# Fewer and longer tiled w4 excursions, padded kv and M products, earlier pq transposes and a longer filler in a matmul-bound mixer kernel

## Chip, cores and metric

One core of one Trainium2 chip. The metric is the device time of one execution in microseconds (us), and the median over the runs is quoted. Engines: PE is TensorE (PEld its weight loads), DVE is VectorE, ACT is ScalarE, POOL is GpSimd, SP issues most DMAs. The profile traces one execution; its span (263.0 us before) is about 2 us shorter than the device time.

## The reference, cut

```python
x = A_x                                            # (1, 2048, 640) bf16
g = sigmoid((x * gate_w).sum(-1, keepdims=True))
# A: linear attention, 32 heads of 20
q, k, v = split(x @ wqkv); pq, pk = phi(q), phi(k)
kv = einsum("bhsd,bhse->bhde", pk, v); z = pk.sum(s)
a = (pq @ kv / (pq . z)) @ wo
# B: token-shift mixer and an MLP of width 1728
h  = gelu(layernorm(x) @ w1); x1 = x + shift(h) @ w2
b  = x1 + gelu(layernorm(x1) @ w3) @ w4
return g * a + (1 - g) * b
```

The sequence is 16 tiles of 128 tokens. The MLP width 1728 is 13 x 128 + 64. Those last 64 rows are the "w4 half": a product that contracts over 64 rows only.

## The kernel before, the parts that matter

The program is recorded by items (`("w3", c, j)` and so on). A small scheduler in Python puts the items in order by a model of time and by stated dependencies; each engine then executes its own list in that order. The 64-row products for two token tiles run at once, one on each half of the array's rows:

```python
    def w4_half(t):                        # called for even t: tiles t and t+1
        ...
        for i in range(2):
            b = pair()                     # two of the eight PSUM banks per tile
            bs += [b, b + 1]
            w4_banks[t + i] = (b, b + 1)
        bank_hold.update(bs)
        for i, (n0, n1) in enumerate(((0, 512), (512, D))):
            for par in range(2):
                rows = slice(64 * par, 64 * par + 64)
                jobs.append((ps[:, bs[2 * par + i], 0:n1 - n0],
                             h2h[rows, t // 4, 128 * pr:128 * (pr + 1)], w4[rows, KFF, n0:n1]))
        ...
    # kvt_group: for the last of six blocks both the stationary and the moving side have 40 columns
    m = min(128, D - R6 * r)               # 128, ..., 40
    mms.append((ps[0:m, b, ...], wv[:, k, R6 * r:R6 * r + m], GT[:, k, R6 * r:R6 * r + n], ...))
    # m_group: the last of six blocks contracts 40 rows, the others 120
    mm_group(ps[:, b, 0:512], [(Lt[0:n, r, :], wo_aug[0:n, r, 0:512])])
    # transposes of the normalized pq tiles: only after the last transpose of xn
    IT.add("QT", ("qt", t), 0.0, ..., deps=[(("qn", t), 3.2), (("w2", NT - 1), 0.5), (("t2", NT - 1), 0.0)])
    # filler products before x arrives, so that the PE clock is released
    NWARM = 5; NWARM2 = 2                  # 512 columns each
```

`w3_half` is the matching 64-column product of w3 (two for the whole sequence). Each w4 tile is followed by an eviction on DVE that adds it to `abx`, which an A tile (`a_tile`, product of pq and M) wrote before.

## Time and profile before

| | before |
|---|---|
| device time, median (range, 6 runs) | 264.98 us (264.82 to 265.63) |
| span of the profiled run | 263.0 us |
| PE busy | 258.2 us, 98% |
| DVE, ACT, POOL busy | 56%, 41%, 35% |

The page of the kernel before: the span, the busy time of each engine, and the chain of work that ended last.

```profile
span 263.0 us, 4293 instructions
PE 258.2 (98%) x1699; PEld 134.9 (51%) x1699; DVE 146.8 (56%) x249; ACT 108.7 (41%) x217; POOL 93.1 (35%) x148
...
PE 88%; DMA 3%; POOL 3%; DVE 3%; ACT 1%; issue 1%; SPq 0%; DVEq 0%; POOLq 0%
```

PE has almost no slack, and nothing else is near it. The list of PE's waits confirms that (who waited for whom: total us, times, longest).

```profile
PE ps L835 <- POOL ones_c L666: 1.6, 1, 1.6
PE ps L607 <- DMA pqnT<-pq_tok: 0.3, 1, 0.3
PE ps L618 <- DMA x_tok<-in_A_x_dram: 0.2, 1, 0.2
```

But the busy time hides small holes, because the traced end of a product reaches into the next one. **Read start to start instead.** In a steady stream a 128x512 product starts 0.216 us before its follower and a 128x128 product 0.056 us before. The PE timeline of the kernel before (start us, duration us, engine, line, operation, names, tile, shape, count; a row merges neighbours of one line and shows the shape of the first), at the kv block, at the 40-row M product, and at the first A tiles with the first w4-half:

```profile
79.33 0.65 PE L937 MATMUL ps<-GT,wv 128*128 128x120 bf16 x10
79.92 2.33 PE L607 MATMUL ps<-xnT,w 128*128 128x512 bf16 x10
...
113.86 0.44 PE L607 MATMUL ps<-wo_aug,Lt 40*128 40x512 bf16 x2
114.23 1.96 PE L607 MATMUL ps<-w,hsT 128*128 128x512 bf16 x12
...
140.09 4.25 PE L607 MATMUL ps<-M_sb,pqnT 128*128 128x512 bf16 x30 [0.31 <-DMA pqnT<-pq_tok]
144.28 0.45 PE L1089 MATMUL ps<-w,h2h 64*128 64x512 bf16 x4
144.65 7.24 PE L1107 MATMUL ps<-w,h2T 128*128 128x512 bf16 x52
```

Fifteen A pairs take 15 x (0.216 + 0.056) = 4.08 us, so the w4-half should start at 144.17; it starts at 144.28. Its four products run as two concurrent pairs, 0.27 us of work; the next group should start at 144.55 and starts at 144.65. So there is a hole of about 0.1 us on the way into the 64-row tiles and another on the way out. The waits list shows neither. The PEld timeline of the kernel before shows the weight load of the new tile at the same place:

```profile
144.27 0.11 PEld L1089 LDWEIGHTS ps<-w,h2h 64*128 64x128 bf16 x4
```

In the steady stream a weight load starts 214 ns (median) before its product, beside the product ahead. Here it starts only 4 ns before its product, 94 ns after the columns of the product ahead have gone through. At all 24 changes of shape in this trace the load is held back like this (by 90 to 95 ns), and the product follows within 5 ns. So the hole is a pause ahead of both, not the time of an uncovered weight load; what goes on in the pause the trace does not show. The 40-row M product takes 0.37 us for 0.27 us of work, with one more hole ahead of it, and the kv block 0.59 us.

### The profile page before, as it was taken

To read this page: it belongs to the slowest core of one execution; us is meant where nothing else is said; L and a number is where in the kernel's file an instruction comes from. 1 tells how busy PE (TensorE), PEld (TensorE's weight loads), DVE (VectorE), ACT (ScalarE), POOL (GpSimd) and SP (SyncE) were. 2 spreads that over 40 slices of the span, in tenths; PEclk is the share of its full clock that TensorE was granted. 3 is DMA by queue.
4 is the path that set the end of the run, shared out by engine and by line. 5 is a ranking of instruction groups with operands and counts; after the bars stand their busy time and mean duration, and the time that the engine had idled before them with its cause. 6 is when DMAs were issued, how large, how long until landed. Compare 5 with 4: busy or idle time off the path is not lost.

```text
span 263.0 us, 4293 instructions
## 1 busy us (share of the span) xinstructions
PE 258.2 (98%) x1699; PEld 134.9 (51%) x1699; DVE 146.8 (56%) x249; ACT 108.7 (41%) x217; POOL 93.1 (35%) x148
## 2 busy tenths in 40 slices
PE   7999999999999999999999999999999999999996
PEld 3555555555555555554444554544555455545553
DVE  0497877899703797989995659611212121212242
ACT  3596677741365757775862013112221222121000
POOL 4013995859764027587861103001120011021020
PEclk9999999999999999999999999999999999999999
DMA  6775989641668896245256651410000200002011
GB/s 212 238 102 140 189 165 159 189 89 27 96 120 110 276 376 106 54 78 78 56 99 124 98 107 25 122 30 0 2 0 0 102 0 0 2 0 100 2 50 50
DMA packets 50675, 24.82 MB, mean 94 GB/s; under 512 B 42036, under 2 KB 49245, under 8 KB 50656
## 3 DMA queue, kind: packets, MB, share of 16 engines
q1 hardware_dynamic: 49408, 21.28, 36.5%
q0 software_dynamic: 1152, 3.28, 5.5%
q8 instruction: 13, 0.21, 0.3%
q14 instruction: 6, 0.05, 0.1%
q10 hardware_dynamic: 96, 0.00, 0.0%
HBM read 12.05 MB, written 2.62 MB: 56 GB/s over the span
## 4 chain that ended last, share of the span: by engine, by line
PE 88%; DMA 3%; POOL 3%; DVE 3%; ACT 1%; issue 1%; SPq 0%; DVEq 0%; POOLq 0%
PE ps L607 53%; PE ps L1107 22%; PE ps L787 8%; PE ps L859 2%; POOL xn L629 1%; DMA x_tok<-in_A_x_dram 1%; PE ps L1089 1%; POOL st L637 1%; DMA pqnT<-pq_tok 1%; DMA xnT<-xn 1%; DVE x_tok L644 1%; PE ps L618 1%; ACT junk L662 1%; PE ps L937 1%; PE ps L860 1%
## 5 line engine op out<-in xcount | busy, mean ns | idle before, releaser
L607 PE MATMUL ps<-xnT,w 128*128 128x512 bf16 x360 | 84.4, 379 | 0.0
L663 ACT ACTIVATE h2T<-ps 128x512 bf16<-128x512 f32 x52 | 31.0, 597 | 85.6 <-PE ps L607 85.6
L1107 PE MATMUL ps<-w,h2T 128*128 128x512 bf16 (+1 forms) x416 | 58.7, 299 | 0.0
L607 PEld LDWEIGHTS ps<-xnT,w 128*128 128x128 bf16 x360 | 33.4, 98 | 33.8 <-ACT M_sb L663 0.4
L629 POOL TENSOR_SCALAR abx<-x_tok,stg 128x640 f32<-128x640 bf16 x16 | 13.3, 834 | 104.5 <-DVE x_tok L646 72.7
L1107 PEld LDWEIGHTS ps<-w,h2T 128*128 128x128 bf16 x416 | 32.4, 98 | 27.8 <-issue 2.1
L646 DVE SCALAR_TENSOR_TENSOR x_tok<-ps,stg,abx 128x640 bf16<-128x640 f32 (+2 forms) x17 | 14.3, 844 | 49.2 <-PE ps L1107 49.2
L629 POOL TENSOR_SCALAR xn<-x_tok,st 128x640 bf16<-128x640 bf16 x32 | 35.5, 1115 | 8.8 <-DMA xnT<-xn 8.3
L646 DVE SCALAR_TENSOR_TENSOR abx<-ps,stg,abx 128x640 f32<-128x640 f32 x16 | 14.1, 883 | 29.4 <-PE ps L607 24.4
L663 ACT ACTIVATE Er<-ps 128x640 bf16<-128x640 f32 x32 | 22.5, 705 | 12.7 <-PE ps L607 8.5
L663 ACT ACTIVATE hsT<-ps 128x512 bf16<-128x512 f32 (+1 forms) x32 | 18.9, 594 | 14.6 <-PE ps L607 14.2
L662 ACT ACTIVATE junk<-x_tok 128x640 bf16<-128x640 bf16 x32 | 23.6, 737 | 1.5 <-DVE x_tok L644 1.2
L607 PE MATMUL ps<-M_sb,pqnT 128*128 128x512 bf16 (+1 forms) x160 | 23.7, 299 | 0.3 <-DMA pqnT<-pq_tok 0.3
L607 PE MATMUL ps<-w,hsT 128*128 128x512 bf16 (+1 forms) x160 | 23.9, 299 | 0.0
L787 PE MATMUL ps<-pk_tok,x_tok 128*128 128x512 bf16 (+1 forms) x160 | 23.9, 299 | 0.0
L607 PE MATMUL ps<-wkg,xT 128*128 128x512 bf16 (+1 forms) x150 | 22.6, 299 | 0.0
L607 PEld LDWEIGHTS ps<-M_sb,pqnT 128*128 128x128 bf16 x160 | 13.1, 98 | 12.8 <-DMA pqnT<-pq_tok 0.8
L607 PEld LDWEIGHTS ps<-w,hsT 128*128 128x128 bf16 x160 | 13.3, 98 | 12.4 <-DVE qprod L637 0.3
L607 PE MATMUL ps<-wq,xT 128*128 128x512 bf16 (+1 forms) x120 | 18.3, 299 | 0.0
L629 DVE TENSOR_SCALAR Er<-Er 128x640 bf16<-128x640 bf16 x32 | 12.0, 376 | 9.4 <-ACT Er L663 8.9
L644 DVE SCALAR_TENSOR_TENSOR x_tok<-ps,x_tok 128x640 bf16<-128x640 f32 x16 | 13.0, 821 | 7.4 <-PE ps L607 5.9
L607 PEld LDWEIGHTS ps<-wkg,xT 128*128 128x128 bf16 x150 | 12.1, 97 | 9.0
(67 smaller groups left out, 229.2 us busy)
## 6 DMA issues: line engine op xcount, KB each, us to landing
w<-in_B_w_dram SPq DMA_DIRECT2D x1, 2160.0 KB, 8.2
w<-in_B_w_dram SPq DMA_DIRECT2D x1, 2080.0 KB, 13.8
x_tok<-in_A_x_dram SPq DMA_DIRECT2D x3, 640.0 KB, 5.8
out_dram<-x_tok SPq DMA_DIRECT2D x3, 640.0 KB, 3.2
w<-in_B_w_dram POOLq DMA_DIRECT2D x8, 160.0 KB, 4.9
wq<-in_A_wqkv_dram SPq DMA_DIRECT2D x5, 160.0 KB, 4.3
wkg<-in_A_wqkv_dram SPq DMA_DIRECT2D x5, 160.0 KB, 4.2
wv<-in_A_wqkv_dram POOLq DMA_DIRECT2D x1, 800.0 KB, 6.5
```

What stands on the lines that cost most here:

```text
L607: ins = e.matmul(out_ap, l, r, start=(i == 0), stop=(i == n - 1))
L618: ins = e.transpose(o, s_, ident[:])
L629: return engf(lambda e: e.tensor_scalar(out_ap, in_ap, s1, s2, op0, op1), rd, [out_ap], cost=cost)
L637: return engf(lambda e: e.tensor_tensor(out_ap, a, b_, op), [a, b_], [out_ap], cost=cost)
L644: return dve(lambda e: e.scalar_tensor_tensor(out_ap, in0, scalar, in1, op0, op1, accum_out=accum), rd, [out_ap, accum], cost=cost + 70.0)
L646: return dve(lambda e: e.scalar_tensor_tensor(out_ap, in0, scalar, in1, op0, op1), rd, [out_ap], cost=cost)
L662: return act(lambda e: e.activation(out_ap, in_ap, func, bias=bias, scale=scale, accum_out=accum), rd, wr, cost=cost)
L663: return act(lambda e: e.activation(out_ap, in_ap, func, bias=bias, scale=scale), rd, wr, cost=cost)
L787: ins = e.matmul(o, l, r, start=(t0 + q_ == 0), stop=(t0 + q_ == NT - 1))
L859: e.matmul(ps[:, b, 0:512], l, w[:, k, 0:512], start=(k == 0), stop=(k == KD - 1))
L860: return e.matmul(ps[:, b + 1, 0:n2], l, w[:, k, 512:512 + n2], start=(k == 0), stop=(k == KD - 1))
L1107: ins = e.matmul(o, l, r, start=False, stop=(i == KFF - 1))
```

## The change

The intent is to take holes out of the PE stream: half as many changes between full and tiled products, no wait before the first A tile, and a filler that runs until x arrives. The diff, cut to its core:

```diff
-    NWARM = 5
-    NWARM2 = 2
+    WARM = 3072                      # columns: six 512-wide products
+    WARM2 = 768                      # 512 + 128 + 128
 ...
-    wv = ra.alloc("wv", [128, KD, D], BF16)
+    wvf = ra.alloc("wv", [128, KD * D + 88], BF16)
+    wv = wvf[:, 0:KD * D].rearrange("p (k d) -> p k d", d=D)
+    memset(pool, wvf[:, KD * D:], 0.0)
+    memset(pool, wo_aug[:, 5, :], 0.0)
 ...  kvt_group
-                mms.append((ps[0:m, b, ...], wv[:, k, R6 * r:R6 * r + m], ...
+                mms.append((ps[:, b, ...], wvf[:, D * k + R6 * r:D * k + R6 * r + 128], ...
 ...  m_group
+        kr = R6 if r < 5 else 128
-        mm_group(ps[:, b, 0:512], [(Lt[0:n, r, :], wo_aug[0:n, r, 0:512])])
+        mm_group(ps[:, b, 0:512], [(Lt[0:kr, r, :], wo_aug[0:kr, r, 0:512])])
 ...  w4_half, now called for t % 4 == 0
+        b0, b2, bt = pair(), pair(), pair()
+        tiles = [((b0, b2)[i // 2] + i % 2, bt + i % 2, 128 * (i // 2)) for i in range(4)]
+        bank_hold.update((b0, b0 + 1, b2, b2 + 1, bt, bt + 1))
+            for pr in range(2):
+                for par, tail in ((0, False), (1, False), (0, True), (1, True)):
 ...  order
-    IT.add("QT", ("qt", t), ..., (("t2", NT - 1), 0.0)])
+    IT.add("QT", ("qt", t), ..., (("t2", 11 if t < 6 else NT - 1), 0.0)])
+            deps.append((("w3", 1, t + 6), 0.0))         # A tile t < 4 after w3 group t + 6
+            deps4.append((("w3", min(c + 1, NCH - 1), KFF - 1), 0.0))
+            deps4.append((("a", t + 3), 0.0))            # w4 tile t after A tile t + 3
+            if c == 0 and j == 3:
+                deps.append((("w2", NT - 1), 0.0))
```

(Cut: every w4 eviction on DVE is now two instructions, since a tile's 512 and 128 columns lie in banks that are not neighbours; the pq normalization follows another pace; further rules for the order of w3 groups and A tiles; the scheduler's own constants.)

## The prediction

> **What bounds the kernel.** TensorE, almost without a break. The page has PE busy 258.2 of 263.0 us (98%) at full granted clock. The list of PE's waits has three entries: 1.6 us for the first memset, 0.3 us for the transpose of pq_tok before the first A tile, 0.2 us for the first x load. The chain of waits gives PE 88%; its DVE/ACT/POOL/DMA part (117 to 140 us) runs beside a busy PE and costs just that 0.3 us. In the PE timeline a 128x512 product follows the last after 216 ns, a 128x128 one after 56 ns. No faster DVE, ACT or POOL can gain; only holes in the PE stream can.
>
> **Holes, from start-to-start times on PE.**
> 1. At each change of operand shape class (full 128x128 against 64-row, 64-column, 40-row or 40-column tiles) the next product starts 94 to 99 ns late; the 120-row products show no such hole. The Trainium skill, "TensorEngine Tiling (Array Packing)", Key Properties, says that switching tiling mode drains the engine; this trace agrees, at about 96 ns a switch. Before has 24: eight w4-half excursions (16), two w3-half (4), the 40-column kv block (2), the 40-row M product (2): about 2.3 us.
> 2. The step before the first A tile, at 139.4 us, is 685 ns in place of 216: 0.47 us lost.
> 3. The start: cold clock up to about 5.3 us, 0.43 us between filler and first transposes, 0.19 us waiting for the ACT copy of xT tile 1.
>
> **What the change does.**
> - Four w4-half excursions instead of eight, with the same products; kv and M padded. By the order of instructions one excursion now directly follows the second w3-half and shares a switch. Left: 2+2+3+2+2 = 11 switches. Removed: 13 x 96 ns = 1.25 us, all on PE's own chain.
> - Inside an excursion there is now a step from one pair's tails to the next pair's mains with new weights: an estimate of 0 to 50 ns each, at most 0.2 us.
> - pq transposes 0 to 5 stand before the last four xn ones, and the first A tile comes after seven w3 groups of chunk 1 instead of five. The transposes land long before: the 0.47 us goes.
> - Six 512-wide fillers at 427 ns end at about 4.1 us, when x lands: the break closes but the transposes start no earlier. The second filler shrinks, but the second q product waits for the ACT copy at 6.1 us anyway. -0.1 to +0.1 us.
> - DVE gets 15 small instructions where it is 20% busy; padding adds no PE columns; two memsets on an idle POOL. Nothing.
> - Six PSUM banks are held per excursion, leaving one pair for the A tile between two w4 tiles. Its eviction (0.88 us, after 0.8 us on POOL) has 3.5 us. I expect no new wait.
>
> **Predicted.** 265.02 - 1.25 - 0.47 + 0.1 = 263.4 us. Range 262.7 to 264.3. Faster by over 2%: 0.01; within 2%: 0.97; slower: 0.02.
>
> **What would show it.** PE busy near 256.5, span near 261.3; four w4-half groups, each with two switch holes (one shared), none around kv and M; no PE wait on pqnT; no new PE wait on DVE or ACT at w4-half or A tiles; the end (1.1 us DVE, then output DMA) unchanged.
>
> **What would make it wrong.** Six held banks making an excursion or an A tile wait 0.5 us for an eviction; weight swaps inside the excursion costing as much as a switch; the last xn transposes, now behind six pq ones, landing late; the clock at the start released earlier or later by the unbroken filler, some 0.3 us either way.

## The result

| | before | after |
|---|---|---|
| device time, median (range, 6 runs each) | 264.98 us (264.82 to 265.63) | 263.64 us (263.45 to 264.65) |
| ratio of fast runs | | 0.9953 (95%: 0.9932 to 0.9974) |
| span of the profiled run | 263.0 us | 261.6 us |
| long stretch of PE (see below) | 248.261 us | 246.835 us |

A ratio is the mean time of one kernel's fast runs over that of the other's fast runs of the same rounds, so not quite the ratio of the medians. "Long stretch" is, here and below, the time on PE from the start of the first k product (near 12 us) to the start of the last product, read from start times in the PE timeline. It leaves out the first 12 us, which turn out to vary from run to run.

The change wins 1.34 us by the medians, half a per cent. The page and the waits of the kernel after:

```profile
span 261.6 us, 4302 instructions
PE 257.2 (98%) x1701; PEld 135.4 (52%) x1701; DVE 147.7 (56%) x264; ACT 108.2 (41%) x217; POOL 95.9 (37%) x150
...
PE 98%; DVE 1%; POOL 0%; ACT 0%; issue 0%; POOLq 0%
```

```profile
PE ps L839 <- POOL ones_c L667: 1.6, 1, 1.6
```

The chain of waits now runs through PE alone (98% in place of 88%), and the pqnT and x waits are gone from the list. The PE timeline of the kernel after, at the places shown of before:

```profile
79.36 0.55 PE L940 MATMUL ps<-GT,wv 128*128 128x120 bf16 x10
79.75 2.32 PE L608 MATMUL ps<-xnT,w 128*128 128x512 bf16 x10
...
114.95 0.43 PE L608 MATMUL ps<-wo_aug,Lt 128*128 128x512 bf16 x2
115.22 1.03 PE L608 MATMUL ps<-w,hsT 128*128 128x512 bf16 x4
...
140.77 1.03 PE L608 MATMUL ps<-xnT,w 128*128 128x512 bf16 x4
141.63 1.52 PE L608 MATMUL ps<-M_sb,pqnT 128*128 128x512 bf16 x10
...
151.82 1.89 PE L608 MATMUL ps<-xnT,w 128*128 128x512 bf16 x8
153.64 0.39 PE L1094 MATMUL ps<-w,h2h 64*128 64x512 bf16 x2
153.87 0.22 PE L1091 MATMUL ps<-w,h2h 64*128 64x128 bf16 x2
153.92 0.38 PE L1094 MATMUL ps<-w,h2h 64*128 64x512 bf16 x2
154.14 0.22 PE L1091 MATMUL ps<-w,h2h 64*128 64x128 bf16 x2
154.29 3.71 PE L1112 MATMUL ps<-w,h2T 128*128 128x512 bf16 x26
...
```

Ten kv products take 0.39 us instead of 0.59, the padded M product 0.27 instead of 0.37, and the first A tile follows its w3 group without a hole (four products from 140.77 end at 141.63). The w4-half for four tiles takes 0.65 us for 0.54 us of work: one hole out (the hole in lies before it) for four tiles. Between its two pairs (153.87 to 153.92) there is no hole at all.

Two things are new. Around the M products PE starts late, without any entry in the waits list:

```profile
127.12 0.52 PE L608 MATMUL ps<-wo_aug,Lt 120*128 120x512 bf16 x2
127.47 1.24 PE L608 MATMUL ps<-xnT,w 128*128 128x512 bf16 x5
128.56 0.44 PE L608 MATMUL ps<-wo_aug,Lt 120*128 120x512 bf16 x2
128.97 1.25 PE L608 MATMUL ps<-xnT,w 128*128 128x512 bf16 x5
```

The pair of 127.12 takes 0.35 us and that of 128.56 0.41 us, for 0.27 us of work each. The weight-load timeline of the kernel after names the wait (in brackets: idle time before, and what ended it), and its ACT timeline shows the reason:

```profile
127.41 0.10 PEld L608 LDWEIGHTS ps<-wo_aug,Lt 120*128 120x128 bf16 x1 [0.39 <-ACT h2T L664]
128.97 0.11 PEld L608 LDWEIGHTS ps<-xnT,w 128*128 128x128 bf16 x2 [0.31 <-ACT M_sb L664]
```

```profile
125.07 0.74 ACT L663 ACTIVATE junk<-x_tok 128x640 bf16<-128x640 bf16 x1 [2.26 <-DVE x_tok L645]
125.71 0.19 ACT L663 ACTIVATION_READ_ACCUMULATOR junk<-x_tok 128x1 f32 x1
125.80 2.52 ACT L664 ACTIVATE h2T<-ps 128x512 bf16<-128x512 f32 x5
```

ACT sat idle for 2.26 us, because the square of the last x1 tile stood next in its list and waited for DVE. Five evictions of w3 groups then came at once, and PE ran out of free banks. The second new wait stands before the fourth w4-half (timeline of all engines, kernel after):

```profile
241.87 1.08 DVE L647 SCALAR_TENSOR_TENSOR x_tok<-ps,stg,abx 128x512 bf16<-128x512 f32 x2 [1.92 <-PE ps L1112]
...
242.67 0.10 PEld L1094 LDWEIGHTS ps<-w,h2h 64*128 64x128 bf16 x2 [0.29 <-DVE x_tok L647]
...
```

It takes three of the four pairs of banks directly after a w4 tile, and must wait until DVE has evicted that tile's 512 columns. That start is 288 ns late, where a mere switch makes 96 to 99.

Adding up the lateness of every product in the long stretch against its columns at 2.4 per ns (the rate that the 0.216 and 0.056 us above show, less about 3 ns each):

| in the long stretch, us | before | after |
|---|---|---|
| steps that change the tile shape: count, sum | 24, 2.32 | 11, 1.06 (+0.19 of bank wait) |
| hole before the first A tile | 0.47 | 0 |
| holes at the M products | 0 | 0.24 |

1.26 + 0.47 - 0.19 - 0.24 = 1.30 of the 1.426 us. The other 0.12 us are small: the first product after a switch is about 10 ns slower than others, and the steps inside the tiled groups that went had been slower too.

### The profile page after: what moved, and what is told of

Its sections match the earlier page's. It is cut to its first block, busy times and chain, and to the rows that moved or that the text cites. A ratio compares the mean times of both kernels' runs of the same rounds, so it can differ in the third digit from the quotient of the medians.

```text
span 261.6 us, 4302 instructions
## 1 busy us (share of the span) xinstructions
PE 257.2 (98%) x1701; PEld 135.4 (52%) x1701; DVE 147.7 (56%) x264; ACT 108.2 (41%) x217; POOL 95.9 (37%) x150
## 4 chain that ended last, share of the span: by engine, by line
PE 98%; DVE 1%; POOL 0%; ACT 0%; issue 0%; POOLq 0%
PE ps L608 61%; PE ps L1112 21%; PE ps L790 8%; PE ps L863 2%; PE ps L839 1%; PE ps L1026 1%; PE ps L1094 1%; DVE x_tok L647 1%; PE ps L619 1%; PE ps L940 1%; PE ps L864 1%; POOL ones_c L667 0%; ACT xT L664 0%; PE ps L1091 0%; POOLq L1254 0%
## 5 line engine op out<-in xcount | busy, mean ns | idle before, releaser
L608 PE MATMUL ps<-xnT,w 128*128 128x512 bf16 x360 | 82.1, 379 | 0.0
L608 PEld LDWEIGHTS ps<-xnT,w 128*128 128x128 bf16 x360 | 34.0, 98 | 36.8 <-ACT M_sb L664 0.3
L630 POOL TENSOR_SCALAR abx<-x_tok,stg 128x640 f32<-128x640 bf16 x16 | 15.3, 958 | 101.3 <-DVE x_tok L647 93.9
L647 DVE SCALAR_TENSOR_TENSOR x_tok<-ps,stg,abx 128x512 bf16<-128x512 f32 (+1 forms) x32 | 17.2, 550 | 60.5 <-PE ps L1112 60.4
L630 POOL TENSOR_SCALAR xn<-x_tok,st 128x640 bf16<-128x640 bf16 x32 | 34.7, 1090 | 16.8 <-DMA xnT<-xn 16.3
L608 PE MATMUL ps<-M_sb,pqnT 128*128 128x512 bf16 (+1 forms) x160 | 24.3, 299 | 0.0
```

Source lines behind the costliest of these rows:

```text
L608: ins = e.matmul(out_ap, l, r, start=(i == 0), stop=(i == n - 1))
L630: return engf(lambda e: e.tensor_scalar(out_ap, in_ap, s1, s2, op0, op1), rd, [out_ap], cost=cost)
L647: return dve(lambda e: e.scalar_tensor_tensor(out_ap, in0, scalar, in1, op0, op1), rd, [out_ap], cost=cost)
```

## Experiments

Each run was set beside the kernel before on the same chip: one chip for the first and third batches, another for the second. All results were correct. The runs came in three batches: e1 to e4; i_sqa, after_again, i_all and i_allw; i_all_again, i_early and i_nofill. In the second, one execution of the kernel before took 267.67 us, which lowers that batch's ratios by about 0.1%. The table has the numbers; the readings follow.

| run | first k product at, us | long stretch, us | span | median time | ratio to before (95%) |
|---|---|---|---|---|---|
| before | 11.90 | 248.261 | 263.0 | 264.98 | |
| after | 11.93 | 246.835 | 261.6 | 263.64 | 0.9953 (0.9932 to 0.9974) |
| after_again | 12.61 | 246.849 | 262.3 | 264.17 | 0.9945 (0.9916 to 0.9975) |
| e1_pad | 11.93 | 247.590 | 262.3 | 264.11 | 0.9971 (0.9953 to 0.9990) |
| e2_qt | 12.49 | 247.784 | 263.1 | 264.58 | 0.9979 (0.9964 to 0.9994) |
| e3_half8 | 11.93 | 248.190 | 262.9 | 264.92 | 0.9998 (0.9982 to 1.0014) |
| e4_fill | 12.35 | 248.253 | 263.4 | 264.93 | 0.9994 (0.9979 to 1.0008) |
| i_sqa | 11.76 | 246.410 | 261.0 | 263.20 | 0.9916 (0.9873 to 0.9958) |
| i_all | 11.60 | 246.186 | 260.6 | 263.29 | 0.9907 (0.9877 to 0.9938) |
| i_all_again | 11.63 | 246.185 | 260.6 | 263.08 | 0.9925 (0.9908 to 0.9941) |
| i_allw | 12.37 | 246.188 | 261.4 | 263.74 | 0.9936 (0.9906 to 0.9966) |
| i_early | 12.35 | 246.185 | 261.3 | 262.96 | 0.9921 (0.9905 to 0.9938) |
| i_nofill | 13.98 | 246.186 | 263.0 | 264.47 | 0.9972 (0.9956 to 0.9988) |

The long stretch repeats within 15 ns, while one kernel's times spread over 0.8 us and more. So the stretch decides about effects of some tenths of a us, and the times confirm them.

**e1_pad: the padding alone, on the kernel before.** The edit is the `wvf`, `memset`, `kvt_group` and `kr` lines of the diff above.

> The kernel before with the padding of the kv and M products alone. Theory (each change of tile shape on PE drains it, about 97 ns for the step into it and about 10 ns for the first product after it): the four switches around the 40-column kv block and the 40-row M product go, the hole at each of these places falls from 94 to 98 ns to about 3 ns, span 263.0 - 0.4 = 262.6 us, time 0.4 us less. Rival (the holes are waits for an eviction or for weights of the new group, which padding leaves in place): holes stay at 94 ns and the span stays at 263.0 us.

The holes at kv and at the 40-row M product are gone, with the same products, dependencies and weights: ten kv products take 79.36 to 79.75 in this trace too. The twenty switch steps left sum to 1.93 us against 2.32 us for 24: 96 ns each. The stretch fell by 0.67 us, more than the 0.4 expected. The rest is the hole before the first A tile, 0.22 us in place of 0.47: the pq transposes were issued 0.64 us earlier than before (136.70 against 137.34 us), and the PE work ahead of the A tile ended only 0.39 us earlier. The theory holds, the rival falls; the surplus, 0.25 us, belongs to another hole.

**e2_qt: the pq transposes alone, on the kernel before.**

```diff
-    ... (("w2", NT - 1), 0.5), (("t2", NT - 1), 0.0)])
+    ... (("w2", NT - 1), 0.5), (("t2", 11 if t < 6 else NT - 1), 0.0)])
```

> The kernel before with the pq transposes 0 to 5 let go after the eleventh xn one alone; PE order otherwise as before. Theory: the 0.47 us hole before the first A tile closes and nothing else moves: span 262.5 us, time 0.5 us less, no PE wait on pqnT. Rival (the hole only turns into another wait there: M_sb, its tail rows, or a late xn transpose): a hole of 0.2 to 0.5 us stays near 140 us and the span is 262.8 to 263.0 us.

The stretch fell by 0.477 us, the size of the hole. No hole is left before the first A tile. PE's order did not stay as it was, which the expectation had wrong: the scheduler now puts the A tiles between earlier w3 groups, the first at 135.9 us. So the run shows what the edit brings together with that order, not the transposes at a fixed order. The span did not fall, for its first k product came 0.6 us later in that execution; the times fell by 0.2%. The expected span was missed for that reason, and the stretch shows the gain.

**e3_half8: the kernel after, with eight excursions.** Same banks, same order, but the second pair's products stand before the third tile.

```diff
-            for pr in range(2):
-                for par, tail in (...):
+            for par, tail in (...):               # pr = (t % 4) // 2
-        if t % 4 == 0:
+        if t % 2 == 0:
             IT.add("W4", ("w4h", t), ...
```

> The kernel after, with its order, banks and padding kept, but the w4-half products of each four tiles done as two excursions of two tiles again (eight excursions). Theory (the gain is the number of switches): eight switches more at about 107 ns each, span 261.6 + 0.86 = 262.4 us, time 0.8 to 0.9 us more than after. Rival (the fixed order and fewer waits give the gain, the excursions are hidden): within 0.2 us of after, span 261.6 to 261.8 us.

The stretch grew by 1.355 us, more than expected. The PE timeline of e3_half8 at one of the added excursions and at the last one:

```profile
162.44 1.52 PE L608 MATMUL ps<-M_sb,pqnT 128*128 128x512 bf16 x10
163.89 0.39 PE L1099 MATMUL ps<-w,h2h 64*128 64x512 bf16 x2
...
164.27 1.04 PE L1117 MATMUL ps<-w,h2T 128*128 128x512 bf16 x4
...
251.36 0.39 PE L1099 MATMUL ps<-w,h2h 64*128 64x512 bf16 x2 [0.45 <-DVE x_tok L647]
```

At 163.89 there are the two usual holes: ten A products from 162.44 end at 163.80, and 0.27 us of tiled work takes 0.38. The last excursion, directly after a w4 tile, waits 0.52 us more for DVE, a wait that this experiment brought in itself. Without it the stretch grew by 0.84 us: 105 ns for each of eight switches. So the number of excursions is worth what the theory says; with the order of the kernel after kept, eight excursions lose it again. The run also shows the second new wait a second time: a w4-half that directly follows a w4 tile waits for that tile's eviction.

**e4_fill: the filler alone, on the kernel before.** The edit is the `WARM` lines of the diff.

> The kernel before with the new filler alone (six 512-wide products, then 768 columns). Theory: the second q product waits for the ACT copy of xT tile 1 as before, so no gain: span 263.0 us within 0.1, time within 0.15 us of before. Rival (the unbroken filler releases the clock earlier, or makes the slower executions, about 0.6 to 1 us longer in both kernels, rarer): clock released before 4.9 us in the trace, or the highest times of the run below 265.2 us.

The stretch is the same within 8 ns, the median 264.93 against 265.20 us, the ratio 0.9994 with 1 inside the interval. The span is 0.4 us longer, since the first k product came later, the clock was released at 6.80 us in its one trace, not before 4.9, and the highest time was 265.33 us. No gain, as predicted. The rival, that an unbroken filler makes the longer executions rarer, found no support: after_again, which has the same filler, gave five of six times between 263.96 and 264.33 us where the result above had four of six at 263.65 us or less (other rounds, and perhaps another chip).

**after_again: where the spread of one kernel comes from.**

> The kernel after, unchanged, to compare on the same chip. Theory: the stretch of PE from the first k product to the last product is 246.84 us again within 0.05, while the first k product itself starts anywhere from 11.9 to 12.5 us, according to when the clock is released; times 263.4 to 264.7 us. Rival (the stretch varies by itself): the stretch differs by over 0.1 us.

The stretch repeated within 14 ns and the start moved by 0.68 us. The PE timeline of after_again, and after it that of i_all (same filler and first products), in the first microseconds:

```profile
5.20 0.85 PE L839 MATMUL ps<-ones_c 128*128 128x512 bf16 x3
5.84 0.63 PE L863 MATMUL ps<-wq,xT 128*128 128x512 bf16 x1
6.27 0.31 PE L864 MATMUL ps<-wq,xT 128*128 128x128 bf16 x1
...
7.71 0.38 PE L863 MATMUL ps<-wq,xT 128*128 128x512 bf16 x1
```

```profile
4.82 0.49 PE L839 MATMUL ps<-ones_c 128*128 128x512 bf16 x3
5.38 0.38 PE L863 MATMUL ps<-wq,xT 128*128 128x512 bf16 x1
5.60 0.22 PE L864 MATMUL ps<-wq,xT 128*128 128x128 bf16 x1
```

In after_again the 128x512 q product lasts 0.63 us and its follower starts 0.43 us later: half rate. In i_all it lasts 0.38 us and its follower starts 0.22 us later. PE ran its last half-rate step until 7.33 us in after_again, 4.33 us in i_all, and in between elsewhere (5.16 before, 5.20 after, 5.62 e1_pad, 5.83 e3_half8, 6.80 e4_fill, 6.99 e2_qt), always with the first product at 1.58 us. The Trainium skill, "TensorE: Matmul & The Clock Gate", Part 1, "What's actually happening", says that the clock is released by a free-running window of 3413 ns, so that the moment varies; the traces agree that it varies: by 3.0 us between i_all and after_again (same filler, batch and chip), and by 2.1 us between two executions of one kernel (after and after_again). That a window causes it is the page's account, which no run here shows. So the start is chance as far as these runs show, and 1.0 us of the time with it.

**i_sqa: the two new waits taken away.**

```diff
-        IT.add("SQ", ("sq", t), 0.0, ..., [(("w2", t), 1.0)])
+        IT.add("SQ", ("sq", t), 0.0, ..., [(("w2", t), 1.0)] + ([(("w3", 0, t - 8), 0.0)] if t >= NT - 2 else []))
+            if t == NT - 4:                         # the fourth w4-half
+                deps4.append((("a", NT - 1), 0.0))  # after the last A tile
```

> The kernel after with two orders changed: the squares of the last two x1 tiles stand later on ACT (after w3 groups 6 and 7), and the last A tile stands before the fourth w4-half. Theory: the two holes at M products near 127 to 129 us (72 and 146 ns) were a queue of h2T evictions behind a square that waited for DVE, and the 288 ns hole before the fourth w4-half was a wait of 190 ns for the eviction of the w4 tile just before; so these holes fall to 3, 3 and 98 ns and the stretch of PE from the first k product to the last product falls from 246.84 to about 246.4 us, time 0.4 us less. Rival (the M holes come from padding or the banks): the M holes stay; only 0.2 us is won.

The stretch fell to 246.410 us, by 0.425 us. The PE timeline of i_sqa at the M products:

```profile
125.07 2.32 PE L608 MATMUL ps<-xnT,w 128*128 128x512 bf16 x10
127.23 0.44 PE L608 MATMUL ps<-wo_aug,Lt 120*128 120x512 bf16 x2
127.50 2.75 PE L608 MATMUL ps<-xnT,w 128*128 128x512 bf16 x11
```

The M pair takes 0.27 us, without a hole, and the fourth w4-half starts 98 ns late like the others. The padding and the number of banks are those of the kernel after, so the rival falls: both waits came from the order of instructions. This trace, and those of after_again, i_all and i_allw, lack some 30 product records, one about every 7 us; each looks like a hole of one product's length, and the same product leaves none in the complete traces (after, i_all_again).

**i_all and i_all_again: the w3-half groups moved together.** On top of i_sqa:

```diff
-        if c % 2 == 0:
-            IT.add("W3", ("w3h", c), 1.27, lambda c=c: w3_half(c), [...])
+        if c == 1:
+            for h in (0, 2):
+                IT.add("W3", ("w3h", h), 1.27, lambda h=h: w3_half(h), [(("t2", NT - 1), 0.9)])
```

> As i_sqa, and both w3-half groups stand together directly before the first w4-half, so five switches do what took seven. Theory: 2 x 107 ns more are won: stretch from the first k product to the last product 246.2 us, time about 0.6 us below after. Rival (the w4-half must now wait for the eviction of h2h or for banks): a hole of 0.3 us or more before the first w4-half, stretch 246.4 us or more.

> As i_all, unchanged, as the base for the next two on the same chip. Theory: the stretch from the first k product to the last product is 246.19 us again within 0.05; the first k product starts anywhere from 11.6 to 12.6 us, with the clock release; times 262.4 to 263.5 us. Rival: the stretch differs by over 0.1 us, so the order is not what set it.

The PE timeline of i_all_again at the merged groups:

```profile
149.76 2.10 PE L608 MATMUL ps<-xnT,w 128*128 128x512 bf16 x9
151.80 2.35 PE L1026 MATMUL ps<-xnT,w 128*64 128x512 bf16 x20
154.08 0.39 PE L1094 MATMUL ps<-w,h2h 64*128 64x512 bf16 x2
...
154.73 1.47 PE L1112 MATMUL ps<-w,h2T 128*128 128x512 bf16 x6
```

Column tiles go straight over to row tiles, and the w4-half does not wait: the second w3-half covers the eviction of the first. The stretch fell to 246.186 us, by 0.224 us for two switches, and repeated at 246.185. Nine switches are left, 0.87 us in all. Over both batches (12 runs) the times are 262.42 to 263.59 us; its ratio to before was 0.9907 where after_again had 0.9945 in the same rounds. **This version beats both kernels, by 2.0 us and 0.9 us by the medians of that batch**, and by 2.08 and 0.65 us by the long stretch, which leaves the chance of the start out. (The intervals of i_all's and after_again's ratios overlap; against the kernel after it is the stretch that decides.) That is still under one per cent.

**i_allw, i_early, i_nofill: the start of the filler**, on i_all. In i_allw DVE sets the ones and the filler is one product longer. In i_early POOL sets the first 256 columns first and the filler reads those. In i_nofill the first filler is left out.

```diff
-    memset(pool, ones_c[:], 1.0)
+    memset(dve, ones_c[:], 1.0)                    # i_allw, with WARM = 3584
+    memset(pool, ones_c[:, 0:256], 1.0); memset(pool, ones_c[:, 256:768], 1.0)   # i_early, WARM = 3328, 256-wide
-    addA(("warm",), 0.0, lambda: warmup(WARM, 0.834))     # i_nofill
```

> As i_all, and the ones that the filler reads are set by DVE instead of POOL, with one filler product more, so PE starts about 0.5 us earlier. Theory[...]: the release comes on average 0.5 us earlier, the first k product at 11.5 to 12.3 us, time 0.2 to 0.3 us below i_all. Rival (the release does not depend on when PE starts): first k product 11.9 to 12.5 us, time as i_all within 0.15 us.

> As i_all, but POOL sets the first 256 columns of ones first and the filler reads only these, so PE starts near 1.2 in place of 1.6 us, and thirteen 256-wide products end when x lands. Theory[...]: with PE busy 0.4 us earlier the release comes 0 to 0.4 us earlier on average, which can win 0.2 us at most[...]: time within 0.25 us of i_all_again. Rival (the filler's start fixes the release): 0.3 us or more.

> As i_all without the first filler, so that PE starts with the transposes at 4.1 us. Theory[...]: release at 6.5 to 10 us instead of 4.3 to 7.4, the first k product at 13 to 14.5 us, time 1.0 to 2.0 us more than i_all_again. Rival (the filler does nothing that the products after it would not do, as e4 would suggest): within 0.3 us.

i_allw failed as an experiment. DVE began its memset at 1.02 us and took 0.70 us, so PE started at 1.78 instead of 1.58 us, and the longer filler ran until 4.74 us, 0.6 us past the arrival of x. It tells nothing of an earlier start. In i_early PE did start at 1.16 us, and the one traced execution was released only at 6.80 us. Its median was 262.96 against 263.08 us: no effect that these rounds can show. i_nofill cost 1.4 us (264.47 against 263.08 us): PE started at 4.19 us with the transposes and ran at half rate until 10.14 us. So the filler is worth 1.4 us, but not its last half microsecond, within what these rounds can tell.

## Why the prediction was right

The time, 263.64 us, lies 0.24 us from the predicted 263.4 and inside the range. The closeness is partly luck: the start alone moves an execution by 1.0 us, and the same kernel gave a median of 264.17 us in after_again, 0.77 us from the prediction. What the terms were worth is read from the stretch. Point by point:

- **"Removed: 13 x 96 ns = 1.25 us, all on PE's own chain."** Right. Switch steps sum to 2.32 us before and 1.06 us after, 96.5 ns each. e1_pad showed it with four of them, e3_half8 with eight, i_all with two. The one shared switch is in the trace of after (column tiles to row tiles at 189 us, 99 ns late).
- **"at most 0.2 us"** for weight swaps inside an excursion. Right on the safe side: no hole.
- **"The transposes land long before: the 0.47 us goes."** Right. e2_qt alone won 0.477 us.
- **"-0.1 to +0.1 us"** for the filler. Right in e4_fill: no effect seen, in a start that varies by 1 us on its own. The prediction had allowed "some 0.3 us either way" for the clock, 0.6 us in all; the first k product moved over 1.0 us.
- **"I expect no new wait."** Wrong, and the largest error among the terms: 0.19 us before the fourth w4-half, and 0.24 us at the M products. The first was among the things named as able to make it wrong. The second was not thought of. The step that failed was to check the places where the diff changed PE, and not the order on ACT: the diff's pace for the pq normalization and its order of the last w2 tiles let a square that waits for DVE stand before evictions in ACT's list. i_sqa shows that moving the squares takes this hole away; which of the two, pace or order, had put them there was not tested apart.
- **"PE busy near 256.5, span near 261.3"**: 257.2 and 261.6. The span is off by 0.3 us, less than the 0.43 us of the new waits (see below); busy time, which counts holes as work, was a poor thing to predict.

The two new waits, 0.43 us, were partly made up by two terms on the other side: the 0.1 us allowed for the start, of which the traces show 0.03, and the 0.12 us of small steps. With what follows it, a switch was worth 105 to 112 ns in e3_half8 and i_all.

## What to carry to other kernels

When one engine is busy 98% of the span, look at start-to-start times of its instructions: the busy time counted the holes at each change of tile shape as work, and the list of waits had none of them. Group the products that use a smaller tile, or pad them if padding adds no columns, and let a different tiled group follow directly rather than go back to the full shape in between. After a reordering, read the in-order lists of the engines that free the buffers too; and judge effects of tenths of a microsecond by a stretch that leaves the start out.

## What the Trainium skill lacked or had wrong

- "TensorEngine Tiling (Array Packing)", Key Properties, says that a change of tiling mode drains the engine, but gives no price. Here the next product and its weight load start late, the product by 96.5 ns on average (24 switches, 2.32 us), about 105 to 112 ns with what follows. A change from column tiles to row tiles costs the same as one to the full shape (99 ns). Products with 120 rows count as full (no hole); ones with 40 rows or 40 columns do not.
- "TensorE: Matmul & The Clock Gate", Part 1, has the release after a busy window of about 3.4 us ("What's actually happening") and the change of rate about 4 us into the activity, 500 ns either way ("What you observe"), though it notes too that the number of slow products varies from run to run. Here the release came from 2.75 us (i_all) to 5.75 us (after_again) after the first product, and 5.95 us without filler. So it can come before 3.4 us of activity have passed, and the spread, 3.0 us, is wider than 500 ns either way and close to the window that the page names.
- The same page, "Back-to-back issue gap", gives 81 ns (128 columns) and 131 ns (512 columns) for sustained streams with a weight load per product. Here such streams ran at 56 and 216 ns, which that page calls the isolated gap.
- "Perfetto Trace Analysis" says that the profiler estimates the end of a product on TensorE. It does not say that this can hide a wait: a product that waits for a semaphore can show no idle time on PE, because the modelled end of the product before covers it. Here the 146 ns hole at the M product appears only as the weight load's 0.31 us wait.
